# Second-group queries placed between the halves of the group one scores, norm sums accumulated by the adds, and nine value steps placed anew

## The chip, the cores and the metric

The kernel runs on one core of one Trainium2 chip. A core has a matrix engine (TensorE, PE in the profile; its weight loads are PEld), a vector engine (VectorE, DVE), a scalar engine (ScalarE, ACT), GpSimd (POOL) and SyncE (SP), whose queue issues the DMAs here. The metric is the device time of one execution in microseconds. A profile is taken of one execution; its span runs from the first to the last instruction.

## What is computed

Two layers of the same block, for four sequences that each decode one token. A block is grouped-query attention over a cache of 4096 positions, then a gated feed-forward network, each behind a layer norm and with a residual.

```python
B, Sq, D = 4, 1, 512
Hq, Hkv, Sk, Dh = 32, 8, 4096, 128            # w_gate, w_up: 512 x 1792; all bf16
def _A_ref(x, k_cache, v_cache, wq, wo):
    q = (x @ wq)                               # 32 heads of 128; 4 query heads share a key head
    scores = einsum("bhqd,bhkd->bhqk", q, k) * (Dh ** -0.5)
    o = einsum("bhqk,bhkd->bhqd", softmax(scores), v)
    return o @ wo
def _B_ref(x, w_gate, w_up, w_down):
    return (_gelu(x @ w_gate) * (x @ w_up)) @ w_down
x = x + _A_ref(_layernorm(x), K, V, wq, wo);  x = x + _B_ref(_layernorm(x), ...)
x = x + _A_ref(_layernorm(x), K, V, wq, wo);  x = x + _B_ref(_layernorm(x), ...)
```

Both layers use the same caches and the same weights. The keys are 33.6 MB and the values 33.6 MB.

## The kernel before

**Stages.** The order of all instructions is written by hand (`manual_schedule`), so what is written first on an engine runs first on it. The first layer's attention goes row by row over the four sequences. The main loop (L624 to L646) has one pass for each row b: the dense stage of the first layer for row b, the norm and queries of the second layer for row b, and then `attend` (L461), which joins the second layer's attention of row b with the first layer's attention of row b+1. In the last pass `attend_last` (L567) has only the second layer's part. A final dense stage does all four rows at once (L648).

**Groups and tiles.** The eight key heads form two groups of four (`groups`, L113; ga comes first, gb second). A cache tile is half the positions of one head, 128 x 2048 bf16, 512 KB. All 16 key tiles of a row stay in SBUF in `KT`, and both layers use them, so keys are read from HBM once. `keys.load` (L333) overwrites a tile with that of the next row; on SP's queue it waits until the second layer's scores have read it. `keys.turn` (L340) transposes each tile in place, on VectorE. `scores` (L351) takes one half (t) of one group: 16 matmuls against `qb`, which `q_build` (L230 on TensorE, L233 on VectorE) fills for one group at a time. `q_rows` (L209) is the query product of a group, 16 matmuls; its rows are transposed by L199 and spread by `q_spread` (L220).

**Values.** Values are read for each layer anew, into seven buffers. A value step (`Values.step`, L432) uses one tile in 16 matmuls (L446), gives its buffer back, and lets `load_v` (L426) put further loads on SP's queue. The order of use is written down in `order`: the second layer's first two tiles of a row (kept in their buffers since the first layer, KEEP), 16 tiles of the next row's first layer, then the other 14 of the second layer. Those 14 steps are left over when `attend` returns; the next pass spends them as `fill(n)` in the dense stage and `rest(n)` in `attend`. While `seen["hold"]` is set, `load_v` issues nothing. In `attend` this keeps value loads behind the key loads on SP's queue.

**Small pieces.** The norm squares x (L154), averages x and its square over partitions with a matmul (L159), reduces the four columns (L161), subtracts the mean (L162), and finds the reciprocal root in ten small steps on VectorE (`ln_rstd`). The dense stage has two input products (`ffn_in`, L285), the gate (`gelu`, `gate_up`, with H_bf at L308) and the down product (L315). `soft` (from L357) is the softmax of a group: maximum, exponential (L370), and then a transpose (L378), 16 products (L397) and a copy to `pe` (L400).

## Time and profile before

| | |
|---|---|
| median of 8 runs | 324.69 us (321.93 to 327.6) |
| the profiled execution | 323.01 us, span 321.2 us |
| moved by DMA | 110.38 MB on SP's queue |
| HBM rate over the span | 344 GB/s |
| mean granted TensorE clock | 0.714 |
| value loads | 112 into value buffers, 8 into key tiles |
| key loads | 64 |

The page shows the span in 40 slices of 8 us. Each digit is a busy share in tenths; the last row is the rate in GB/s.

```profile
PE   1460576334675369879854488998444888976964
...
DVE  5576750023458894254488943544789434533134
...
DMA  6999999999949999998999999999999999899910
GB/s 250 399 412 406 407 410 396 350 387 374 361 118 406 400 396 330 302 376 285 285 414 408 411 406 385 338 318 319 403 411 409 406 395 344 266 327 357 406 41 3
```

From left to right: the first row's attention up to about 50 us, then the weights' loading, and from 84 us on the main loop. The low slice at 88 to 96 us lies between the dense stage of row 0 and the first loads of the next row's keys. Similar, shallower places come near 150, 210 and 280 us. The last two slices are the final dense stage, with nothing left to load.

### The profile page before, as it was taken

Reading aid. Unit: us, or ns where it says so; the run is one execution under the profiler, and the core shown is the slowest. Engines: PE = TensorE matmul, PEld = TensorE weight load, DVE = VectorE, ACT = ScalarE, POOL = GpSimd, SP = SyncE. Lnnn points to the kernel's source line nnn. Section 1 sums busy time; section 2 is a strip of 40 time slices with the busy share of each in tenths; the row PEclk is TensorE's granted clock in tenths of the full one; section 3 lists DMA queues with packets and bytes.
Section 4 is the critical chain, followed back from the end, with each engine's and each line's share of the span. In section 5 each row is a group of like instructions: output and inputs, shape, how many; then the busy total and the mean of one; then the engine's idle time right before and its main releaser. Section 6 shows DMA issues by size and latency. Waiting matters only on the chain.

```text
span 321.2 us, 8609 instructions
## 1 busy us (share of the span) xinstructions
PE 208.5 (65%) x3812; PEld 120.6 (38%) x3812; DVE 172.1 (54%) x459; ACT 29.0 (9%) x70; POOL 0.7 (0%) x6
## 2 busy tenths in 40 slices
PE   1460576334675369879854488998444888976964
PEld 0010245121332046645520256665202565635542
DVE  5576750023458894254488943544789434533134
ACT  0002010000010103000201012001011120004000
POOL 0000000000000000000000000000000000000000
PEclk9999999999997555576955555559555555578557
DMA  6999999999949999998999999999999999899910
GB/s 250 399 412 406 407 410 396 350 387 374 361 118 406 400 396 330 302 376 285 285 414 408 411 406 385 338 318 319 403 411 409 406 395 344 266 327 357 406 41 3
DMA packets 34646, 110.94 MB, mean 345 GB/s; under 512 B 3112, under 2 KB 9008, under 8 KB 34608
## 3 DMA queue, kind: packets, MB, share of 16 engines
q1 hardware_dynamic: 34608, 110.38, 92.2%
q8 instruction: 30, 0.49, 0.6%
q14 instruction: 8, 0.07, 0.0%
HBM read 110.37 MB, written 0.00 MB: 344 GB/s over the span
## 4 chain that ended last, share of the span: by engine, by line
DMA 58%; PE 25%; DVE 7%; SPq 6%; issue 2%; ACT 1%; ACTq 0%
DMA kt<-in_A_k_cache_dram 25%; DMA v<-in_A_v_cache_dram 25%; PE sc L351 7%; PE ot L446 6%; DMA wd_sb<-in_B_w_down_dram 5%; PE rows L209 3%; DMA kt<-in_A_v_cache_dram 3%; DVE kt L340 3%; SPq L126 3%; PE rows L285 2%; PE y L315 2%; PE rows L264 2%; SPq L333 1%; PE y L270 1%; SPq L127 1%
## 5 line engine op out<-in xcount | busy, mean ns | idle before, releaser
L340 DVE STREAM_TRANSPOSE kt<-kt 128x1024 f32<-128x1024 f32 x64 | 76.2, 1223 | 9.4 <-DMA kt<-in_A_k_cache_dram 8.9
L446 PEld LDWEIGHTS <-v 128*128 128x128 bf16 x1920 | 60.4, 104 | 54.7 <-DMA v<-in_A_v_cache_dram 30.6
L446 PE MATMUL ot<-pe,v 128*128 128x4 bf16 x1920 | 64.3, 166 | 23.5 <-DMA v<-in_A_v_cache_dram 19.9
L351 PE MATMUL sc<-kt,qb 128*32 128x512 bf16 x512 | 59.8, 518 | 20.9 <-DVE kt L340 18.3
L351 PEld LDWEIGHTS <-qb 128*32 128x32 bf16 x512 | 17.2, 110 | 49.1 <-issue 24.5
L199 DVE STREAM_TRANSPOSE rows<-rows 128x512 f32<-128x512 f32 (+1 forms) x25 | 17.5, 702 | 27.2 <-PE rows L264 15.2
L453 DVE TENSOR_TENSOR OT_bf<-ot,rden 128x8 bf16<-128x8 f32 x32 | 5.4, 170 | 41.6 <-PE ot L446 34.9
L370 ACT ACTIVATE pp<-sc,nm 128x512 bf16<-128x512 f32 x16 | 11.0, 688 | 157.2 <-DVE junk L366 127.7
L397 PE MATMUL x<-pp,ident_bf 128*32 128x128 bf16 x256 | 9.1, 283 | 23.3 <-DVE pp L378 23.2
L209 PE MATMUL rows<-wq_sb,xn_bf 128*1 128x512 bf16 (+1 forms) x160 | 17.5, 589 | 5.3 <-DMA wq_sb<-in_A_wq_dram 4.7
L264 PE MATMUL rows<-wo_sb,OT_bf 128*1 128x512 bf16 (+1 forms) x120 | 14.8, 614 | 6.6 <-DMA wo_sb<-in_A_wo_dram 6.3
L397 PEld LDWEIGHTS <-ident_bf 128*32 128x32 bf16 x256 | 6.7, 121 | 29.4 <-issue 27.3
L357 DVE TENSOR_REDUCE m<-sc 128x1 f32<-128x512 f32 x16 | 10.8, 675 | 12.6 <-PE sc L351 12.6
L378 DVE STREAM_TRANSPOSE pp<-pp 128x512 bf16<-128x512 bf16 x16 | 11.2, 702 | 5.6 <-ACT pp L370 5.3
L233 DVE TENSOR_TENSOR qb<-qe,amask 128x256 bf16<-128x256 f32 x16 | 6.8, 422 | 10.2 <-PE qe L230 10.2
L400 ACT CAST pe<-x 128x512 bf16<-128x512 f32 x16 | 9.4, 586 | 21.9 <-PE x L397 21.9
L315 PE MATMUL y<-H_bf,wd_sb 128*128 128x1 bf16 (+1 forms) x280 | 8.2, 165 | 3.9 <-DVE H_bf L308 2.3
L285 PE MATMUL rows<-wg_sb,xn_bf 128*1 128x448 bf16 (+1 forms) x80 | 8.3, 567 | 3.0 <-DMA wg_sb<-in_B_w_gate_dram 2.4
L285 PE MATMUL rows<-wu_sb,xn_bf 128*1 128x448 bf16 (+1 forms) x80 | 8.1, 556 | 2.9 <-DMA wu_sb<-in_B_w_up_dram 2.9
L315 PEld LDWEIGHTS <-wd_sb 128*128 128x128 bf16 x280 | 7.8, 102 | 5.6 <-DMA wd_sb<-in_B_w_down_dram 3.5
L276 DVE TENSOR_TENSOR XX<-XX,y 128x4 f32<-128x4 f32 (+1 forms) x10 | 1.6, 160 | 15.5 <-PE y L315 9.1
L230 PE MATMUL qe<-qm,t_bf 128*128 128x64 bf16 x16 | 3.3, 208 | 9.1 <-DVE rden L388 5.0
(66 smaller groups left out, 122.5 us busy)
## 6 DMA issues: line engine op xcount, KB each, us to landing
v<-in_A_v_cache_dram SPq DMA_DIRECT2D x112, 512.0 KB, 8.3
kt<-in_A_k_cache_dram SPq DMA_DIRECT2D x64, 512.0 KB, 10.5
wq_sb<-in_A_wq_dram SPq DMA_DIRECT2D x2, 2048.0 KB, 11.2
wo_sb<-in_A_wo_dram SPq DMA_DIRECT2D x4, 1024.0 KB, 11.9
kt<-in_A_v_cache_dram SPq DMA_DIRECT2D x8, 512.0 KB, 9.3
wg_sb<-in_B_w_gate_dram SPq DMA_DIRECT2D x1, 1792.0 KB, 13.5
wu_sb<-in_B_w_up_dram SPq DMA_DIRECT2D x1, 1792.0 KB
wd_sb<-in_B_w_down_dram SPq DMA_DIRECT2D x2, 896.0 KB, 16.6
```

Source lines behind the costliest of these rows:

```text
L199: nc.vector.transpose(out=rows[:, :n], in_=rows[:, :n])
L209: nc.tensor.matmul(rows[j * QS:j * QS + nb, :], lhsT=xn_bf[:, k, bs], rhs=w, start=(k == 0), stop=(k == KD - 1))
L264: nc.tensor.matmul(rows[r0:r0 + lhsT.shape[-1], :], lhsT=lhsT, rhs=wo_sb[:, i, :], start=(at == 0 and n < QD), stop=(at == 2 and n >= hp - ...
L285: nc.tensor.matmul(rows[j * QS:j * QS + nb, :KF * QS], lhsT=xn_bf[:, k, bs], rhs=w[:, j], start=(k == 0), stop=(k == KD - 1))
L315: nc.tensor.matmul(y[:, k], lhsT=wd_sb[:, c, k * P:(k + 1) * P], rhs=H_bf[:, c, :], start=(c == 0 and k == 0), stop=(c == KF - 1), skip_gr ...
L340: nc.vector.transpose(out=words, in_=words)
L351: nc.tensor.matmul(sc[s * QS:(s + 1) * QS], lhsT=qb[:, w0:w0 + 2 * W], rhs=kt[:, :, be // 2, :, be % 2], start=(t == 0 and be == 0), stop= ...
L357: nc.vector.tensor_reduce(out=m[:], in_=sc.rearrange("p c j -> p (c j)"), axis=AX.X, op=ALU.max)
L370: nc.scalar.activation(out=pp[:], in_=sc[:], func=ACT.Exp, bias=nm[:, 0:1], scale=scale, accum_out=ls[:])
L378: nc.vector.transpose(out=flat, in_=flat)
L397: nc.tensor.matmul(x[a * QS:(a + 1) * QS, s], lhsT=ident_bf[:, s * QS:(s + 1) * QS], rhs=pT[:, a], start=True, stop=True, skip_group_check ...
L446: nc.tensor.matmul(self.ot[:, s % 2], lhsT=v[:, i, :], rhs=pe[:, s, c, :], start=(c == 0), stop=(c == C - 1), skip_group_check=True)
```

## The change

The change has three parts. It moves work and leaves the amounts of scores, values and loads as they were.

- **Order.** `last_q`, which built the second group's `qb` behind both halves of the group ga scores, becomes `next_q`: the product of the second group's queries (L209) and what follows it are no longer issued in the main loop but between the two halves of the group ga scores, with `q_build` behind the second half. The hold is set before the first scores. It stops only tiles of the next row's first layer; the second layer's own tiles may still load. The 14 left-over value steps were 10 ahead of `attend` (6 in `dense`, 4 behind it) and 4 in it; they are now 9 (5 and 4) and 5. In the dense stage both input products follow each other, two steps stand ahead of the down product and one behind it. Behind the first group's query product there are two steps, and one more behind its `q_build`.
- **Norm sums.** For one row, the add and the square become `scalar_tensor_tensor` with `accum_out`, so that the matmul of the norm averages two columns. The mean is read as a scalar from its result, and a copy to `mv` stands behind the subtraction.
- **Buffers.** `p1p`, the pool of the first layer's `pe`, has one buffer instead of two. A tile `sums` of two columns is added.

```diff
-    p1p = ctx.enter_context(tc.tile_pool(name="p1p", bufs=NG))
+    p1p = ctx.enter_context(tc.tile_pool(name="p1p", bufs=1))
...
     def ln_square(b0, nb):
         bs = slice(b0, b0 + nb)
-        nc.vector.tensor_tensor(out=XX[:, 1, bs], in0=XX[:, 0, bs], in1=XX[:, 0, bs], op=ALU.mult)
+        if nb == 1:
+            nc.vector.scalar_tensor_tensor(out=XX[:, 1, b0], in0=XX[:, 0, b0], scalar=1.0,
+                                           in1=XX[:, 0, b0], op0=ALU.mult, op1=ALU.mult,
+                                           accum_out=sums[:, 1:2])
+        else:
...
     def ln_center(b0, nb):
         bs = slice(b0, b0 + nb)
+        mv = small.tile([P, 2, nb], FP32, name="mv", tag="mv")
+        if nb == 1:
+            st = ps_sm.tile([P, 2, 1], FP32, name="st", tag="sm")
+            nc.tensor.matmul(st.rearrange("p s o -> p (s o)"), lhsT=mean_f[:, :], rhs=sums[:],
+                             start=True, stop=True)
+            nc.vector.tensor_scalar(out=xn_bf[:, :, b0], in0=XX[:, 0, b0], scalar1=st[:, 0],
+                                    scalar2=None, op0=ALU.subtract)
+            nc.vector.tensor_copy(out=mv[:], in_=st[:])
+            return mv
...
     def add_y(b0, nb, y):
         bs = slice(b0, b0 + nb)
...
+        if nb == 1:
+            nc.vector.scalar_tensor_tensor(out=XX[:, 0, b0], in0=XX[:, 0, b0], scalar=1.0,
+                                           in1=y[:, :, 0], op0=ALU.mult, op1=ALU.add,
+                                           accum_out=sums[:, 0:1])
+        else:
...
     def load_v():
-        while not seen["hold"] and free and seen["load"] < seen["upto"]:
-            b, g, s, t = loads[seen["load"]]
+        while free and seen["load"] < seen["upto"]:
+            b, last, g, s, t = loads[seen["load"]]
+            if seen["hold"] and not last:
+                return
...
         if two:
...
-            for t in range(NT):
-                scores(sc2[0], ga, t)
-                keys.load(GH)
-            last_q()
             seen["hold"] = True
-            rest(2)
+            scores(sc2[0], ga, 0)
+            keys.load(GH)
+            qm1 = next_q()
+            scores(sc2[0], ga, 1)
+            keys.load(GH)
+            q_build(qm1, gb)
+            rest(1)
             for t in range(NT):
                 scores(sc2[1], gb, t)
                 keys.load(GH)
-            rest(1)
             seen["hold"] = False
             load_v()
             p0 = soft(sc2[0])
-            rest(1)
+            rest(2)
             soft_turn(p0)
             pe0, den0 = soft_swap(p0, p2p), soft_den(p0)
+            rest(2)
...
-    def attend_last(b2, last_q, rest):
+    def attend_last(b2, next_q, rest):
...
-        for t in range(NT):
+        def freed(t):
             scores(sc2[0], ga, t)
             free[:0] = [KT[ga * GH + s][t] for s in range(GH)]
             load_v()
-        last_q()
-        rest(2)
+
+        freed(0)
+        qm1 = next_q()
+        freed(1)
+        q_build(qm1, gb)
+        rest(1)
         p0 = soft(sc2[0])
         for t in range(NT):
             scores(sc2[1], gb, t)
         rest(2)
         soft_turn(p0)
         prob2[ga] = (soft_swap(p0, p2p), soft_recip(soft_den(p0)))
+        rest(2)
...
     def dense(b0, nb, proj, fill):
         out_proj_end(*proj)
         y = proj[0]
+        fill(1)
         add_y(b0, nb, y)
         ln_square(b0, nb)
-        fill(1)
         mv = ln_center(b0, nb)
         fill(1)
         rg = ffn_in(b0, nb, wg_sb)
-        rstd = ln_rstd(nb, mv)
-        sq, h = gelu(nb, rg, rstd)
+        ru = ffn_in(b0, nb, wu_sb)
+        sq, h = gelu(nb, rg, ln_rstd(nb, mv))
+        H_bf = gate_up(nb, sq, h, ru)
+        fill(2)
+        y = down(nb, H_bf)
         fill(1)
-        ru = ffn_in(b0, nb, wu_sb)
-        H_bf = gate_up(nb, sq, h, ru)
-        fill(3)
-        y = down(nb, H_bf)
         add_y(b0, nb, y)
...
         dense(b, 1, proj, fill)
         ln_square(b, 1)
-        fill(1)
         mv = ln_center(b, 1)
         fill(1)
+        ga, gb = groups(b + 1)
+        qr0 = q_rows(b, 1, ga)
         rstd = ln_rstd(1, mv)
...
-        ga, gb = groups(b + 1)
-        qr0 = q_rows(b, 1, ga)
+        qm0 = q_spread(turn_rows(qr0, 512)[:, :, 0], am, ga)
+        fill(2)
+        q_build(qm0, ga)
         fill(1)
-        qm0 = q_spread(turn_rows(qr0, 512)[:, :, 0], am, ga)
-        qr1 = q_rows(b, 1, gb)
-        fill(1)
-        q_build(qm0, ga)
-        qm1 = q_spread(turn_rows(qr1, 512)[:, :, 0], am, gb)
+
+        def next_q():
+            return q_spread(turn_rows(q_rows(b, 1, gb), 512)[:, :, 0], am, gb)
+
         if b < B - 1:
-            proj, prev = attend(b, b + 1, lambda: q_build(qm1, gb), fill)
+            proj, prev = attend(b, b + 1, next_q, fill)
         else:
-            proj = attend_last(b, lambda: q_build(qm1, gb), fill)
+            proj = attend_last(b, next_q, fill)
```

More of the change, by code (lines that the diff above doesn't have):

```diff
@@ L94 @@
     XX = state.tile([P, 2, B, KD], FP32, name="XX")
+    sums = state.tile([P, 2], FP32, name="sums")
     OT_bf = state.tile([P, Hq], BF16, name="OT_bf")
@@ L153, in ln_square @@
         bs = slice(b0, b0 + nb)
-        nc.vector.tensor_tensor(out=XX[:, 1, bs], in0=XX[:, 0, bs], in1=XX[:, 0, bs], op=ALU.mult)
+        if nb == 1:
[3 more added lines that the diff above has]
+        else:
+            nc.vector.tensor_tensor(out=XX[:, 1, bs], in0=XX[:, 0, bs], in1=XX[:, 0, bs],
+                                    op=ALU.mult)
     def ln_center(b0, nb):
         bs = slice(b0, b0 + nb)
+        mv = small.tile([P, 2, nb], FP32, name="mv", tag="mv")
[7 more added lines that the diff above has]
+            return mv
         st = ps_sm.tile([P, 2, nb, KD], FP32, name="st", tag="sm")
         nc.tensor.matmul(st[:], lhsT=mean_f[:, :], rhs=XX[:, :, bs], start=True, stop=True)
-        mv = small.tile([P, 2, nb], FP32, name="mv", tag="mv")
         nc.vector.tensor_reduce(out=mv[:], in_=st[:], axis=AX.X, op=ALU.add)
@@ L275, in add_y @@
         bs = slice(b0, b0 + nb)
-        nc.vector.tensor_tensor(out=XX[:, 0, bs], in0=XX[:, 0, bs],
-                                in1=y.rearrange("p k b -> p b k"), op=ALU.add)
+        if nb == 1:
[3 more added lines that the diff above has]
+        else:
+            nc.vector.tensor_tensor(out=XX[:, 0, bs], in0=XX[:, 0, bs],
+                                    in1=y.rearrange("p k b -> p b k"), op=ALU.add)
     def ffn_in(b0, nb, w_sb):
@@ L415 @@
     assert all(u in keep for u in [(0,) + w[2:] for w in value_order(0, 0)[VB - KEEP:]])
-    loads = [(u[0],) + u[2:] for u in order if not (u[1] and (u[0],) + u[2:] in keep)]
+    loads = [u for u in order if not (u[1] and (u[0],) + u[2:] in keep)]
     free = [kvin.tile([P, CH, Dh], BF16, name=f"v{i}") for i in range(KV_BUFS)]
@@ L459, in pairs, with attend @@
         return [(order[n][2] * GH + order[n][3] // 2 * 2) * rep for n in range(0, VB, 2 * NT)]
-    def attend(b2, b1, last_q=None, rest=None):
+    def attend(b2, b1, next_q=None, rest=None):
         two, first = b2 is not None, b1 == 0
```

## The prediction

> **What bounds the kernel now.** First the page, for the bound; then the busy time by stretches, for where that bound is not reached; then the timeline of one such place. A "pass" is one turn of the loop over the four batch rows (row 0 to 3).
>
> ```profile
> PE 208.5 (65%) x3812; PEld 120.6 (38%) x3812; DVE 172.1 (54%) x459; ACT 29.0 (9%) x70; POOL 0.7 (0%) x6
> ...
> q1 hardware_dynamic: 34608, 110.38, 92.2%
> ...
> DMA 58%; PE 25%; DVE 7%; SPq 6%; issue 2%; ACT 1%; ACTq 0%
> ...
> v<-in_A_v_cache_dram SPq DMA_DIRECT2D x112, 512.0 KB, 8.3
> ```
>
> The cache stream bounds it: 110.38 MB, and 58% of the chain that ended last. In its good stretches it runs at about 410 GB/s, 1.28 us for a 512 KB tile. The stretches (last three columns: granted clock, DMA share, GB/s) show where it doesn't:
>
> ```profile
> 176.00:180.00 4.00, 1.77 (x35) 1.41 (x34) 3.58 (x7) 1.34 (x4) 0.00 (x0) 0.50 1.03 409
> 204.00:208.00 4.00, 4.00 (x62) 1.53 (x60) 2.93 (x16) 0.21 (x1) 0.00 (x0) 0.50 0.96 345
> 208.00:212.00 4.00, 3.87 (x126) 3.73 (x123) 1.39 (x6) 0.00 (x0) 0.00 (x0) 0.50 0.92 315
> 212.00:216.00 4.00, 3.96 (x61) 1.74 (x65) 2.92 (x15) 0.00 (x0) 0.00 (x0) 0.52 0.96 305
> 220.00:224.00 4.00, 3.35 (x84) 2.20 (x81) 1.96 (x8) 1.09 (x3) 0.00 (x0) 1.00 0.90 275
> 276.00:280.00 4.00, 3.85 (x61) 1.99 (x62) 2.83 (x16) 0.00 (x0) 0.00 (x0) 0.50 0.78 225
> ```
>
> From 204 to 216 (dense stage, pass of row 2) TensorE is full and DMA is at three quarters: five free value buffers come back only as TensorE uses them, and the next row's keys can't load before scores of the second layer have read their tiles. That point ends the stretch:
>
> ```profile
> 209.46 1.63 PE L315 MATMUL y<-H_bf,wd_sb 128*128 128x1 bf16 x56
> 212.65 1.87 PE L209 MATMUL rows<-wq_sb,xn_bf 128*1 128x512 bf16 x16
> 214.97 1.47 PE L209 MATMUL rows<-wq_sb,xn_bf 128*1 128x512 bf16 x16
> 217.52 2.05 PE L351 MATMUL sc<-kt,qb 128*32 128x512 bf16 x32 [0.54 <-DVE qb L233]
> 218.64 17.12 SPq L333 DMA_DIRECT2D kt<-in_A_k_cache_dram  x16
> 226.35 1.25 DVE L340 STREAM_TRANSPOSE kt<-kt 128x1024 f32<-128x1024 f32 x1 [2.03 <-DMA kt<-in_A_k_cache_dram]
> 283.81 3.41 PE L351 MATMUL sc<-kt,qb 128*32 128x512 bf16 x32 [0.54 <-DVE qb L233]
> ```
>
> To see: both query products precede the first score; key loads start 1.1 us after it. These loads start at 90.94, 153.72 and 218.64; in the last pass (values into key tiles) at 285.53. The spacings, 62.8, 64.9 and 66.9 us, carry 46 tiles each (16 key, 30 value), 58.9 us at 1.28. So 4, 6 and 8 us a pass are open; nothing else here is worth as much.
>
> **Part 1, queries and value steps.** Second-group products go behind the first half of the group one scores, and nine value steps instead of ten stand ahead of it, elsewhere. Pass of row 2, by the timeline. The two L285 blocks (1.66 each) now follow each other, ending near 207.1; two value steps (0.5 each, tiles landed at 205 and 206.4) fill to 208.1. The down product needs H_bf, and that hangs on the DVE chain: from xn_bf (ends 204.0) to H_bf (ends 209.03) is 5.0, of which 0.34 waited for the second L285; the chain without it, plus a copy of 0.2 that the norm edit adds, gives H_bf at about 208.7. Down starts 0.75 earlier than 209.46. From xn_bf of the second norm to the first score it was 4.9 (212.60 to 217.52). It becomes the reciprocal-root chain 2.2, copy 0.2, transpose 0.73, spread 0.22, TensorE product 0.25 and L233 0.42: 4.05, 0.85 saved; the L209 block (1.47 to 1.87) and one value step (0.5) leave the path, so DVE is what is left on it. With 0.2 to 0.4 gained about the norms, key loads start 2.0 us earlier. Pass of row 1: the same order, and it now waits 1.9 us for values (0.49, 0.72, 0.68 idle at 141.6, 142.9, 144.1) in three steps in a row that are spread out: 3.5 earlier. Pass of row 3: a value wait of 1.54 at 282.67 also goes: 3.8 earlier. Row 0 has no value steps to place: 0.85 less the norm edit, 0.6.
>
> Every value step brings its DMA issue. SP's queue holds, in order, four key loads, then (after 1.5 to 1.8 us of L209 and 1.0 of scores) four more, then eight. Four tiles are 5.1 us of transfer and the last values are still on their way, so that hole is covered; if only two were, it would cost about 1 us. The hold now begins earlier, but nine steps free exactly what the pass's last values need (5 + 9 = 14 tiles), so the next layer's first value tile, until now loaded ahead of the keys, comes behind them. Its 1.28 us is given back in each of passes 1 to 3. Can the freed buffers feed the new bunches of two? A value tile lands 5.6 to 8.5 us after its issue at 200 to 218 us; the step pair after the first-group product uses tiles issued 6 us before. Taking 6 (median 6.6), the price is 0 to 0.6; at 8.5 it is 2.
>
> Clock: the row of 283.81 has 3.41 us for 32 scores, where the granted clock was 0.54; the row of 217.52 has 2.05, at 1.00. In this kernel the clock rose at 215.4 and 151 while two L209 blocks ran nearly back to back. The Trainium skill (TensorE: Matmul & The Clock Gate, section "Part 1: The HAM clock gate") says that full clock is granted after a window of about 3.4 us of sustained activity. The trace agrees only where wide matmuls follow each other: 204 to 215 is full of instructions and stays at 0.50. (The L285 blocks, now adjacent, may raise the clock, but 8 us ahead of the scores; a rise at 140.4 was over by 144.6.) With the blocks parted, by the rule read as "busy" the scores keep 2.05 and cost nothing; by the row they cost 0.7 in the half ahead of the key loads, in passes 1 and 2 (pass 3 pays already, pass 0 is at 1.00). I take 0.5, nearer to the row.
>
> What I can't see is the start of the key stream: 220 to 224 ran at 275 GB/s just as 16 key issues pile up, and 288 to 292 at 265. Parted issues could ease it, up to 1.4 us a pass, or leave it; I count 0.3.
>
> **Part 2, norm sums.** Eight one-row norms. The nearest row for the accumulating form is L366: 163 ns and an 82 ns read-out, twice per norm. The 167 ns reduce leaves xn_bf's path; xn_bf takes a pointer scalar (L633: 228 against 169), and a copy (L245: 175) moves behind it. The matmul of two columns instead of eight is priced like L159, 357. Sum per norm on the way to xn_bf: +164 - 197 + 59, nothing; on the root chain +0.2, counted above. Bounds: -0.2 to +0.2 a norm.
>
> **Part 3, one p1p buffer.** The second group's copy must wait for the first group's eight value steps; these stand ahead of its 16 L397 products on TensorE, so the wait is over: zero. If that order did not hold, it would cost at most the 0.59 of L400 per pass.
>
> **Sum.** Key loads earlier, less the value tile, the clock, and plus the start: row 1: 3.5 - 1.3 - 0.5 + 0.3 = 2.0; row 2: 2.0 - 1.3 - 0.5 + 0.3 = 0.5; row 3: 3.8 - 1.3 - 0 + 0.3 = 2.8, of which I drop 1.0, as DMA ran at 225 at 276 to 280 without a reason I can name. Row 0's 0.6 is lost to rival A. Together 4.3; less 0.3 for value waits, 4.0. The final dense stage (308 to the end, 3 GB/s) keeps its order and saves nothing. The profiled execution took 323.01 (span 321.2): 319.0. The median of the runs is 324.69, 1.7 above it; the forecast for the median is 320.7.
>
> **Rivals.** A: the gain is swallowed by DVE. The first group's softmax now stands behind the second L209 block and behind L233 of the second group, 1.5 us later after the first score. On DVE it precedes all key transposes (64 of 1.22), which run nearly full: in row 0's pass 21.3 busy of 24 us (96 to 120). Against: before the first transpose DVE waited for its tile 0.72 (row 1) and 2.03 (row 2). In row 0's pass 0.45 and 0.56 of waits further on absorb most. If this eats the earlier start, the net is 0 to -2: 323 to 324.7.
>
> B: slower. Same place, one price: the scores drop to half clock and the first score is not earlier, because the bunched value steps wait for tiles (8.5 us landings). Then softmax begins 1.7 + 1.8 + 1.7 = 5.2 after the first score instead of 2.05, so the first key transpose slips by 3.2 less the 0.72 or 2.03 of slack, and the last pass slips its exponentials too: 2.5 + 1.2 + 1.5, with 0.3 in row 0: 5.5, 330. It decides where the first score comes less than about 1.2 us earlier (row 2) or 2.5 (row 1). Against: the DVE chain above gives 2.0 and 3.5.
>
> C: the steps weren't moved into gaps, since TensorE has none at 204 to 216, and the value supply sets the pace: no change, 324 to 325.
>
> **How the numbers follow.** The count as made: 0.57, 317.5 to 322.7, mostly beyond 1%. A and C together: 0.26, within 1%. B: 0.12, slower. A stronger gain than counted (start of the key stream eased as well): 0.05, 315 to 317. The range 317.0 to 326.0 leaves out B and the strongest gain. About 1% (3.2 us) is what a measurement of this kernel tells from no change. Faster by over 1%: 0.45 of the first case and 0.05: 0.50; slower 0.12; within 1% 0.38.
>
> **What would show it.** Right: first key loads of the passes some 2 to 4 us earlier after the first value step of the dense stage; the spacings near 63 instead of 65 to 67; DMA above 345 GB/s in the dense stage. Clock: L351 blocks of 16 at 1.0 or 1.7 us, at 1.00 or 0.50. A: the first L340 of a pass starts with no wait for its DMA. B: value steps idle for DMA between L209 and L351. Part 2 is wrong if L276 with its read-out takes more than 0.3. The forecast as a whole is wrong if the spacings shrink but V waits after 120, 185 and 250 grow by as much.

## The result, and the profile after

| | before | after |
|---|---|---|
| median | 324.22 us (318.65 to 327.6, 32 runs) | 318.82 us (317.27 to 322.12, 11 runs) |
| profiled execution | 323.01, span 321.2 | 318.83, span 317.0 |
| mean granted TensorE clock | 0.714 | 0.702 |

The ratio is 0.9911, with a 95% interval from 0.9876 to 0.9947. It counts, of each kernel, only the runs within 1.5% of its own fastest one (13 of the 32 before, 10 of the 11 after), while the medians count all, so it is nearer to 1 than the ratio of the medians (0.983). The kernel is faster, by 0.5 to 1.2% on that ratio. The forecast was 320.7 for the median, with a range of 317.0 to 326.0.

The page of the changed kernel, in its first parts: busy shares, slices of 7.9 us, the DMA queue, and the chain of work that ended last.

```profile
PE 211.1 (67%) x3812; PEld 121.1 (38%) x3812; DVE 170.2 (54%) x475; ACT 28.9 (9%) x70; POOL 0.7 (0%) x6
...
PE   1460585343576667899954588999645788897864
...
DVE  5575751014348895454498933544889344534133
...
GB/s 256 384 412 396 411 409 403 350 379 383 392 112 365 407 407 312 312 358 330 351 405 408 410 408 406 365 283 359 414 409 409 407 388 347 290 291 415 404 46 3
...
q1 hardware_dynamic: 34608, 110.38, 92.5%
...
DMA 49%; PE 21%; DVE 18%; SPq 6%; issue 3%; ACT 1%; ACTq 0%
...
v<-in_A_v_cache_dram SPq DMA_DIRECT2D x112, 512.0 KB, 8.3
```

The bytes are the same and the low places of the last row are still there: 312 near 119 to 135, 283 near 206 to 214, and 290 and 291 near 270 to 285. VectorE's share of the chain went from 7% to 18%. Stretches of the passes of row 2 and row 3 show the same places closer (columns: stretch in us, its length, busy time of PE, PEld, DVE, ACT and POOL with their counts, then granted clock, DMA share, GB/s):

```profile
204.00:208.00 4.00, 3.59 (x113) 3.05 (x105) 1.84 (x11) 0.21 (x1) 0.00 (x0) 0.50 0.79 283
208.00:212.00 4.00, 3.65 (x66) 2.11 (x66) 2.98 (x16) 0.00 (x0) 0.00 (x0) 0.50 0.83 258
212.00:216.00 4.00, 3.86 (x49) 1.76 (x53) 0.49 (x2) 0.00 (x0) 0.00 (x0) 0.50 1.00 355
220.00:224.00 4.00, 2.71 (x90) 2.32 (x83) 1.82 (x4) 1.42 (x4) 0.00 (x0) 0.96 1.01 387
276.00:280.00 4.00, 3.42 (x65) 1.86 (x66) 1.43 (x4) 0.00 (x0) 0.00 (x0) 0.50 0.86 274
```

From 204 to 212, which is the dense stage before its first score, the stream runs at 258 to 283 GB/s: no better than before. The stretch of 220 to 224 runs at 387 instead of 275, but it lies 5.2 us behind the first key load here and 1.4 us behind it before; stretches cut at the first key load follow further down. The gain is not where the kernel is slowest; it is behind it. The timeline of the pass of row 2:

```profile
205.70 1.65 PE L335 MATMUL y<-H_bf,wd_sb 128*128 128x1 bf16 x56 [0.28 <-DVE H_bf L328]
208.83 1.88 PE L224 MATMUL rows<-wq_sb,xn_bf 128*1 128x512 bf16 x16
212.87 1.90 PE L371 MATMUL sc<-kt,qb 128*32 128x512 bf16 x16
214.56 1.92 PE L224 MATMUL rows<-wq_sb,xn_bf 128*1 128x512 bf16 x16
214.79 16.24 SPq L353 DMA_DIRECT2D kt<-in_A_k_cache_dram  x16
216.26 1.35 PE L371 MATMUL sc<-kt,qb 128*32 128x512 bf16 x16
218.29 1.99 PE L371 MATMUL sc<-kt,qb 128*32 128x512 bf16 x32
223.14 1.23 DVE L360 STREAM_TRANSPOSE kt<-kt 128x1024 f32<-128x1024 f32 x1
```

One query product precedes the first score, the other stands between the two halves. The first half of the scores takes 1.90 us for 16 matmuls, where 32 took 2.05 before, so the key loads start 1.92 us after the first score and not 1.12. The first key transpose has no wait in brackets: VectorE comes later than its tile.

A ledger of the whole span, worked out from the two timelines. A pass is cut at the end of the output product (L270 before, L285 after) and at its first key load (in the last pass: the first value load into a key tile). In the lines of rows 1 to 3, the first number is output product to key load, the second is key load to the next output product.

| us | before | after | difference |
|---|---|---|---|
| start to output product of row 0 | 69.82 | 70.14 | +0.32 |
| row 0: output product to key load | 21.12 | 21.46 | +0.34 |
| row 0: key load to next output product | 45.03 | 45.12 | +0.09 |
| row 1 | 17.75 / 48.77 | 14.63 / 48.50 | -3.12 / -0.27 |
| row 2 | 16.15 / 48.76 | 14.94 / 49.33 | -1.21 / +0.57 |
| row 3 (second part: to the end) | 18.13 / 35.67 | 15.64 / 37.24 | -2.49 / +1.57 |

Key loads come 6.82 us earlier over three passes, 1.87 of it is given back behind them and 0.75 is lost up to row 1: 4.20, the difference of the spans. Behind the key loads one value tile more has to be carried in each of these passes (nine value loads precede them, not ten). Three tiles would be 3.84 us at 1.28. That less is given back is mainly due to the first 10 us of the key stream. Before:

```profile
153.72:163.72 10.00, 7.04 (x166) 4.63 (x158) 4.76 (x13) 1.67 (x4) 0.00 (x0) 0.87 0.98 314
218.64:228.64 10.00, 6.30 (x164) 4.39 (x155) 4.52 (x13) 1.67 (x4) 0.00 (x0) 0.87 0.96 331
285.53:295.53 10.00, 7.64 (x179) 4.85 (x171) 4.25 (x15) 2.76 (x7) 0.00 (x0) 0.84 0.93 318
```

And after:

```profile
151.35:161.35 10.00, 7.86 (x189) 4.93 (x182) 5.45 (x16) 1.67 (x4) 0.00 (x0) 0.97 1.00 368
214.79:224.79 10.00, 8.00 (x171) 4.62 (x164) 5.03 (x14) 1.67 (x4) 0.00 (x0) 0.84 1.00 372
279.76:289.76 10.00, 8.89 (x207) 5.49 (x200) 5.01 (x17) 2.08 (x5) 0.00 (x0) 0.84 0.99 345
```

Against the 410 GB/s of a good stretch, 10 us at 314, 331 and 318 lose 2.3, 1.9 and 2.2 us of transfer; at 368, 372 and 345 they lose 1.0, 0.9 and 1.6. That is 3.0 us over the three passes; the 3.84 less these 3.0 would give back 0.86, so about 1.0 us more is lost somewhere else, and the ledger does not say where.

Counted in transfer, the start weighs even more. From output product to key load the kernel before had:

```profile
135.97:153.72 17.75, 15.01 (x305) 9.15 (x306) 9.27 (x45) 0.21 (x1) 0.00 (x0) 0.67 0.94 333
202.49:218.64 16.15, 15.17 (x305) 9.25 (x306) 9.26 (x45) 0.21 (x1) 0.00 (x0) 0.59 0.96 341
267.40:285.53 18.13, 15.74 (x306) 9.19 (x306) 9.26 (x45) 0.21 (x1) 0.00 (x0) 0.59 0.91 320
```

That is 17.2 MB in 52.0 us, and 14.8 MB in 45.2 us after (348, 320 and 312 GB/s, shown below). Against 410 GB/s, 10.0 us of transfer were lost there before and 9.2 after. So of the 6.82 us by which the keys come earlier, only 0.8 is transfer that is no longer lost; the rest, 4.7 tiles, is carried later. That is more than the three tiles counted above, and the 1.0 us can have gone there. The start of the key stream brings 3.0 of the 4.20. Both are read from one execution of each kernel.

### The profile page after: what moved, and what is told of

It is laid out like the page before. It is cut to its first block, busy times and chain, and to the rows that moved or that the text cites. A ratio compares the mean times of both kernels' runs of the same rounds, so it can differ in the third digit from the quotient of the medians.

```text
span 317.0 us, 8624 instructions
## 1 busy us (share of the span) xinstructions
PE 211.1 (67%) x3812; PEld 121.1 (38%) x3812; DVE 170.2 (54%) x475; ACT 28.9 (9%) x70; POOL 0.7 (0%) x6
## 4 chain that ended last, share of the span: by engine, by line
DMA 49%; PE 21%; DVE 18%; SPq 6%; issue 3%; ACT 1%; ACTq 0%
DMA v<-in_A_v_cache_dram 25%; DMA kt<-in_A_k_cache_dram 15%; PE sc L371 6%; DMA wd_sb<-in_B_w_down_dram 5%; DVE kt L360 5%; PE ot L468 5%; DMA kt<-in_A_v_cache_dram 3%; SPq L127 3%; PE y L335 2%; PE rows L224 2%; DVE rows L214 2%; PE rows L279 2%; DVE qb L248 1%; PE st L168 1%; PE x L417 1%
## 5 line engine op out<-in xcount | busy, mean ns | idle before, releaser
L468 PEld LDWEIGHTS <-v 128*128 128x128 bf16 x1920 | 59.8, 104 | 47.7 <-DMA v<-in_A_v_cache_dram 24.3
L468 PE MATMUL ot<-pe,v 128*128 128x4 bf16 x1920 | 63.5, 166 | 20.4 <-DMA v<-in_A_v_cache_dram 17.0
L360 DVE STREAM_TRANSPOSE kt<-kt 128x1024 f32<-128x1024 f32 x64 | 74.1, 1211 | 4.0 <-DMA kt<-in_A_k_cache_dram 4.0
L371 PE MATMUL sc<-kt,qb 128*32 128x512 bf16 x512 | 63.0, 540 | 15.7 <-DVE kt L360 14.0
L371 PEld LDWEIGHTS <-qb 128*32 128x32 bf16 x512 | 17.0, 115 | 46.5 <-issue 37.0
L224 PE MATMUL rows<-wq_sb,xn_bf 128*1 128x512 bf16 (+1 forms) x160 | 18.5, 610 | 4.8 <-DMA wq_sb<-in_A_wq_dram 4.4
L279 PE MATMUL rows<-wo_sb,OT_bf 128*1 128x512 bf16 (+1 forms) x120 | 14.8, 614 | 6.8 <-DMA wo_sb<-in_A_wo_dram 6.6
L305 PEld LDWEIGHTS <-xn_bf 128*1 128x1 bf16 (+1 forms) x160 | 4.6, 113 | 13.3 <-issue 12.1
```

Source lines behind the costliest of these rows:

```text
L224: nc.tensor.matmul(rows[j * QS:j * QS + nb, :], lhsT=xn_bf[:, k, bs], rhs=w, start=(k == 0), stop=(k == KD - 1))
L279: nc.tensor.matmul(rows[r0:r0 + lhsT.shape[-1], :], lhsT=lhsT, rhs=wo_sb[:, i, :], start=(at == 0 and n < QD), stop=(at == 2 and n >= hp - ...
L305: nc.tensor.matmul(rows[j * QS:j * QS + nb, :KF * QS], lhsT=xn_bf[:, k, bs], rhs=w[:, j], start=(k == 0), stop=(k == KD - 1))
L360: nc.vector.transpose(out=words, in_=words)
L371: nc.tensor.matmul(sc[s * QS:(s + 1) * QS], lhsT=qb[:, w0:w0 + 2 * W], rhs=kt[:, :, be // 2, :, be % 2], start=(t == 0 and be == 0), stop= ...
L468: nc.tensor.matmul(self.ot[:, s % 2], lhsT=v[:, i, :], rhs=pe[:, s, c, :], start=(c == 0), stop=(c == C - 1), skip_group_check=True)
```

## The experiments

Three questions: which part of the change pays; what eases the start of the key stream; and whether the new order has room left. "Start" below is the rate in the first 10 us from the first key load, for rows 1, 2 and 3.

### The norm sums, taken out and put in alone

The first kernel is the changed one with the old norm, the second is the kernel before with the new norm and the one `p1p` buffer. Of the first one's edit, the add (the square and the mean go back in the same way):

```diff
...
     def add_y(b0, nb, y):
         bs = slice(b0, b0 + nb)
-        if nb == 1:
-            nc.vector.scalar_tensor_tensor(out=XX[:, 0, b0], in0=XX[:, 0, b0], scalar=1.0,
-                                           in1=y[:, :, 0], op0=ALU.mult, op1=ALU.add,
-                                           accum_out=sums[:, 0:1])
-        else:
-            nc.vector.tensor_tensor(out=XX[:, 0, bs], in0=XX[:, 0, bs],
-                                    in1=y.rearrange("p k b -> p b k"), op=ALU.add)
+        nc.vector.tensor_tensor(out=XX[:, 0, bs], in0=XX[:, 0, bs],
+                                in1=y.rearrange("p k b -> p b k"), op=ALU.add)
```

> The changed kernel without the norm edit: the add, the square, the four-column average and the reduce as before; the order and the one p1p buffer as changed. My reading (the norm edit is worth nothing on the path): within 0.3% of the changed kernel, so about 0.988 of the kernel before by the medians (318.8 to 320). Rival (the edit gives the gain, as it shortens the chain to xn_bf in eight norms): 1 us or more slower than the changed kernel, 320 to 322. A third: the read-outs and the copy cost 0.2 a norm on the root chain, then this is 1 to 1.5 us faster, 317.5.

> The kernel before with the norm edit and the one p1p buffer alone, order as before. My reading: no change, 0.997 to 1.003 of the kernel before. The rival that the norm sums carry the gain expects 0.99. Were the single p1p buffer a wait, it would be slower by up to 0.6 us in each of four passes, 1.007.

Order alone: 319.37 us (6 runs; the kernel before had 324.41 there), ratio 0.9851 (0.9786 to 0.9917). Within its interval that is the whole gain. Norms alone: 323.53 (17 runs) against 324.41, ratio 0.9899 (0.9856 to 0.9942). Here medians and ratio disagree: the medians are 0.3% apart, as I expected, and the ratio, which rests on 8 of the 17 runs, says 1%, as the rival did. Since the change without the norm sums loses nothing, I read them as worth nothing in the new order; that they help in the old one isn't excluded.

### The second product back ahead of the scores, and the product alone moved

The first of these is the changed kernel with both query products back to back:

```diff
         qr0 = q_rows(b, 1, ga)
+        qr1 = q_rows(b, 1, gb)
...
-            return q_spread(turn_rows(q_rows(b, 1, gb), 512)[:, :, 0], am, gb)
+            return q_spread(turn_rows(qr1, 512)[:, :, 0], am, gb)
```

> The changed kernel with the second group's L209 block put back directly behind the first group's, ahead of all scores; the value steps and all else as changed. Clock: with the blocks paired the L351 blocks of the second layer's first group should run at about 1.0 us per half again (1.9 in the changed kernel) and the granted clock be 1.00 there. Time, theory 1 (the changed kernel gains because its key loads go out in parted bunches, so that the key stream starts at a higher rate): the two halves are again 1 us apart, the 10 us from the first key issue fall back from 0.9 to 1.6 us of lost transfer to 1.9 to 2.4, and 2 to 4 us of the gain go: 321 to 323. Theory 2 (it gains because the first score comes earlier): the product adds 1.5 ahead of it and the clock gives 0.85 back, so 0.6 a pass, 2 us in all: 320.5 to 321, with the key stream starting as in the changed kernel.

It took 322.76 (22 runs; the kernel before 324.41), ratio 1.0005 (0.9977 to 1.0034): by the ratio nothing of the gain is left, by the medians 1.7 of 5 us. And not for late keys, which in sum are no later: they start 14.57, 15.91 and 14.65 us behind the output product, against 14.63, 14.94 and 15.64. In rows 1 and 3 the clock is at 1.00, and they follow the first score in 1.09 us instead of 1.92. The stretches from output product to key load of this kernel:

```profile
136.36:150.93 14.57, 13.83 (x290) 8.53 (x290) 9.04 (x48) 0.21 (x1) 0.00 (x0) 0.72 0.90 314
201.70:217.61 15.91, 15.04 (x289) 8.94 (x290) 9.03 (x48) 0.21 (x1) 0.00 (x0) 0.61 0.85 272
269.20:283.85 14.65, 13.92 (x290) 8.44 (x290) 9.04 (x48) 0.21 (x1) 0.00 (x0) 0.71 0.86 292
```

And of the changed kernel:

```profile
136.72:151.35 14.63, 13.47 (x273) 8.24 (x274) 8.17 (x46) 0.21 (x1) 0.00 (x0) 0.62 0.97 348
199.85:214.79 14.94, 13.92 (x273) 8.68 (x274) 8.16 (x46) 0.21 (x1) 0.00 (x0) 0.50 0.90 320
264.12:279.76 15.64, 13.98 (x274) 8.70 (x274) 8.17 (x46) 0.21 (x1) 0.00 (x0) 0.50 0.89 312
```

With the same nine value loads, the stream runs at 314, 272 and 292 GB/s instead of 348, 320 and 312. In transfer lost against 410 that is 13.0 us instead of 9.2 over three passes. The 1.9 us product stands ahead of three value steps, so their buffers come back later: counted from the output product, the last three value loads ahead of the keys begin to be issued at 12.55, 13.01 and 12.62 us in the three rows, against 11.09, 11.40 and 12.11 in the changed kernel. Its place matters for the buffers more than for the first score. Late buffers need not be all of it: in row 2 the DMA share of 0.85 would carry 349 GB/s at the 410 of a full stream, and 272 were moved, so the packets took longer too.

The other one is the kernel before with only the product moved between the halves (value steps, hold and norm as they were):

```diff
-            for t in range(NT):
-                scores(sc2[0], ga, t)
-                keys.load(GH)
-            last_q()
+            scores(sc2[0], ga, 0)
+            keys.load(GH)
+            qm1 = last_q()
+            scores(sc2[0], ga, 1)
+            keys.load(GH)
+            q_build(qm1, gb)
...
```

> The kernel before with one thing changed: the second group's L209 block, its transpose and its spread stand between the two halves of the group ga scores, its q_build behind them. Ten value steps, their places, the hold and the norms as before. The run with the products paired lost 4 of the 5.5 us, so if the parts add up, this one alone carries them: 320 to 321 (0.988 to 0.991 of the kernel before). Rival (it only gains together with the value steps, which then free their buffers without a second product in between): the first score comes 1.5 us earlier in three passes, the half clock gives 0.85 back, and the softmax comes 1 us later after the first score: 322.5 to 324 (0.994 to 1.0).

320.06 (6 runs; the kernel before 323.62), ratio 0.9887 (0.9828 to 0.9945). This one step of the change brings 3.6 us by the medians, where the changed kernel on the same chip brings 4.7. Key loads come 1.2 and 2.2 us earlier in rows 1 and 3, and 0.2 later in row 2. Its start is eased as in the changed kernel (366, 345 and 374):

```profile
153.97:163.97 10.00, 8.43 (x179) 4.87 (x172) 5.38 (x15) 1.67 (x4) 0.00 (x0) 0.84 0.99 366
217.45:227.45 10.00, 8.42 (x165) 4.69 (x158) 5.01 (x14) 1.67 (x4) 0.00 (x0) 0.80 1.00 345
281.97:291.97 10.00, 8.46 (x195) 5.34 (x187) 4.75 (x16) 2.13 (x5) 0.00 (x0) 0.96 1.01 374
```

### What eases the start: the key issues, or distance between the halves

The kernel before with only the places of its key loads on SP's queue changed: four behind the first half of group one, four behind the first half of group two and eight behind its second half. The last pass (row 3) is not touched.

```diff
-            for t in range(NT):
-                scores(sc2[0], ga, t)
-                keys.load(GH)
+            scores(sc2[0], ga, 0)
+            keys.load(GH)
+            scores(sc2[0], ga, 1)
             last_q()
...
-            for t in range(NT):
-                scores(sc2[1], gb, t)
-                keys.load(GH)
+            scores(sc2[1], gb, 0)
+            keys.load(GH)
+            scores(sc2[1], gb, 1)
+            keys.load(2 * GH)
```

> The kernel before, with only the place of key loads on SP's queue changed: four behind the first half of the group ga scores as before, the next four behind the first half of the second group (2 to 3 us later instead of 1), the last eight behind its second half. Scores, queries, norms and value steps as before. Theory 1 (piled key issues slow the start of the stream): the lost transfer in the 10 us from the first key issue falls from 2.2 to about 1.2 in each of the first three passes, 2 to 3 us in all, 0.990 to 0.994 of the kernel before. Theory 2 (the start is slow for another reason, scores running at the same time or fewer tiles under way): no change, or slower by up to 1 us as keys come later: 0.998 to 1.003.

323.41 (22 runs), ratio 0.9989 (0.9961 to 1.0018). The start is 312 and 317 GB/s in rows 1 and 2: no better than 314 and 331. (The 284 of row 3 belongs to an order that is as before, where the first profile had 318: so much can one place vary.) The edit also brings the later keys later, and the DMA share is 0.91 and 0.93 instead of 0.98 and 0.96; but even at a full share, an estimate from these rows, the rates would be 343 and 341, against 368 and 372 in the changed kernel. So parting the issues, by which I had argued for the easing in the forecast, does not bring it about. In this profile the clock was 0.50 at the first scores in all three rows, so a slow first half alone does not ease the start either.

Then the kernel before with two value steps put between the halves, in the place where the change has the product (the hold set earlier, so that they issue no load):

```diff
-            for t in range(NT):
-                scores(sc2[0], ga, t)
-                keys.load(GH)
+            seen["hold"] = True
+            scores(sc2[0], ga, 0)
+            keys.load(GH)
+            rest(2)
+            scores(sc2[0], ga, 1)
+            keys.load(GH)
             last_q()
-            seen["hold"] = True
-            rest(2)
...
```

> The kernel before with one thing changed: the two value steps that stood behind the last scores of the first group now stand between its two halves (both query products stay ahead of the first score, back to back; the hold is set before the scores, so the steps issue no load there, as before). Question: why the start of the key stream is eased (10 us from the first key issue lose 0.9 to 1.6 us of transfer where the second product stands between the halves, 1.9 to 2.4 in the kernel before, and 2.3 to 3.1 with only the places of the key issues changed). Theory 1, mere distance: what counts is that the first eight key tiles are not asked for within 2 us while the last values still arrive. Then the two steps (about 1 us of TensorE) between the halves ease it too, to 1.0 to 1.7 us lost, and the time falls by 1 to 2 us, to about 322. Theory 2, the product: what counts is that one product less stands ahead of the first score, so that the first key issue comes at a better time against the last values. Then the loss stays at 1.9 to 2.6 and the time at 323 to 324.5.

324.48 (22 runs; the kernel before 323.88), ratio 0.9996 (0.9965 to 1.0028), and a start of 329, 327 and 328. About a microsecond of other work between the halves is not enough. What is left is the product: one that is no longer ahead, or one (1.9 us) that is between. The runs don't part these two. The kernel with the products paired ahead of the scores starts at 347, 359 and 358, within what the moved product shows: so something in the other edits eases the start as well, or the dip has only moved out of the 10 us that are looked at.

### Fewer steps ahead, with the products paired in the gap

The changed kernel with both products ahead, where value steps had stood, and two of the nine steps moved behind the group one scores, so that TensorE has less ahead of them.

```diff
             scores(sc2[0], ga, 1)
             keys.load(GH)
+            rest(2)
             q_build(qm1, gb)
...
         qr0 = q_rows(b, 1, ga)
+        qr1 = q_rows(b, 1, gb)
...
-        fill(2)
         q_build(qm0, ga)
...
```

> The changed kernel with both L209 blocks paired again, but in the place of the two value steps that stand behind the first block; these two go behind the group ga scores. So seven value steps instead of nine stand ahead of the first score. If the first score is bound by the VectorE chain (about 4.0 us from xn_bf), it stays where it is in the changed kernel or comes 0.5 later, with the clock at 1.00 and both halves done within 2.1 us. Theory A (when the key loads go out, and the clock, decide): key issues 0.5 earlier, softmax 2 us earlier, 0.5 to 1 us a pass, 316 to 318. Theory B (value buffers that come free ahead of the key issue decide, since only transfers that are under way by then count): two frees later, each pass loses 0.5 to 1.5 us, 320.5 to 323, with more transfer lost between the output product and the key issue than in the changed kernel (2.2 to 3.7 us).

339.24 (6 runs; before 323.62), ratio 1.0506 (1.0453 to 1.0558): far worse. The first score came as early as hoped (13.23, 13.15 and 12.87 us behind the output product). In the pass of row 1 of its timeline:

```profile
150.63 5.56 SPq L353 DMA_DIRECT2D kt<-in_A_k_cache_dram  x8
...
158.15 1.61 SPq L448 DMA_DIRECT2D v<-in_A_v_cache_dram  x2
160.71 9.29 SPq L353 DMA_DIRECT2D kt<-in_A_k_cache_dram  x8
168.37 0.58 PE L468 MATMUL ot<-pe,v 128*128 128x4 bf16 x16 [11.58 <-DMA v<-in_A_v_cache_dram]
...
170.52 1.23 DVE L360 STREAM_TRANSPOSE kt<-kt 128x1024 f32<-128x1024 f32 x1
```

The second layer's last two value tiles are issued behind eight key loads, at 158.15. TensorE works in order and stops 11.58 us at the step that needs the first of them, and the first key transpose starts 19.9 us behind the first key load (7.93 in the changed kernel). Nine steps ahead of the scores, with five free buffers, are exactly the 14 tiles of the second layer. Nine can't be seven.

### Room in the changed kernel

Ahead of the down product TensorE idles 0.28 us for H_bf. One step moved there, from behind the first query product (nine in all, as before the edit):

```diff
-        fill(2)
+        fill(3)
         y = down(nb, H_bf)
...
-        fill(2)
+        fill(1)
         q_build(qm0, ga)
```

> The changed kernel with one value step moved: three instead of two ahead of the down product, one instead of two behind the first query product (nine ahead of the scores, as before this edit). In the changed kernel TensorE idles 0.28 to 0.36 us ahead of the down product for H_bf. Theory 1, that idle time is real room: the step fills it, its buffer comes back some 3 us earlier, and key loads start up to 0.3 us earlier per pass: 318 to 318.9, a ratio to the changed kernel of 0.997 to 1.0. Theory 2, the chain: the step is 0.5 us, 0.2 longer than the room, so down and the second norm come 0.2 us later, and the idle time moves to behind the first query product, where TensorE then waits for VectorE's spread: no change or up to 0.3 us later per pass, 319 to 320.

321.88 (21 runs; the kernel before 323.88), ratio to the kernel before 0.9949 (0.9919 to 0.9978), where the changed kernel has 0.9911: worse than both expectations. The profiled execution took 324.44, so only its order of work is read, in row 2:

```profile
208.31 1.55 PE L335 MATMUL y<-H_bf,wd_sb 128*128 128x1 bf16 x56
...
210.90 0.56 PE L168 MATMUL st<-sums,mean_f 128*128 128x2 f32 x2 [0.63 <-DVE XX L156]
...
214.94 0.24 PE L245 MATMUL qe<-qm,t_bf 128*128 128x64 bf16 x1 [0.72 <-DVE qm L235]
215.97 0.58 PE L468 MATMUL ot<-pe,v 128*128 128x4 bf16 x16 [0.80 <-DMA v<-in_A_v_cache_dram]
```

The wait for H_bf is gone, and others have grown behind it: 0.63 for the norm (none in row 2 of the changed kernel) and 0.72 for the spread (0.47 there), and alike in rows 1 and 3; in row 2 there is also 0.80 for a value tile. The idle time was not room; it only went elsewhere. How much of the loss of time that explains is not shown. The start was 326, 345 and 322 GB/s although the product stands between the halves; since this execution was one of the longest, that decides nothing.

The changed kernel was run twice more, on other chips, for its own spread:

> The changed kernel again, on the chip of the two beside it, as their measure: 318 to 320.

318.94 (6 runs; before 323.62), ratio 0.9879 (0.9828 to 0.9929); start 382, 398 and 386 GB/s, better than in the first profile.

> The changed kernel itself once more, on the same chip as the kernel with row 0's products paired, to compare the two directly and to have a third profile of the start of the key stream. Both theories: 318 to 319.5, 10 us from the first key issue lose 0.3 to 1.6 us of transfer in rows 1 to 3; a profile with more than 2 us lost there would say that the eased start is not a property of this order but varies from run to run.

318.96 (6 runs; before 324.64), ratio 0.9847 (0.9796 to 0.9899); start 394, 403 and 332 GB/s. The 332 loses 1.9 us, more than the 1.6 expected: the eased start varies from run to run with the same order.

Last, row 0 alone with both products ahead. Row 0 has no value steps, and the ledger has its key loads 0.34 us later than before.

```diff
+        if b == 0:
+            qr1 = q_rows(b, 1, gb)
...
+        if b == 0:
+            qm1 = q_spread(turn_rows(qr1, 512)[:, :, 0], am, gb)
...
+            if b == 0:
+                return qm1
             return q_spread(turn_rows(q_rows(b, 1, gb), 512)[:, :, 0], am, gb)
```

> The changed kernel, but in the pass of row 0 alone the second group's query product is issued as in the kernel before: right behind the first group's, both ahead of the first score (row 0 has no value steps to place, so nothing else differs). Question: was row 0's pass made worse by the change (rival A of the forecast, VectorE as the bound, and the half clock in the first half of its scores), or is it neutral? Theory 1, rival A holds in row 0: there VectorE runs full behind the first key tiles; the softmax of the first group comes 1.5 us later in the changed kernel (first key transpose 6.55 us behind the first key issue instead of 4.48), and the next output product ended 0.75 us later (136.72 against 135.97). Then this kernel ends that product near 136.0 and is 0.7 to 1.0 us faster than the changed one: about 318.0, ratio to it 0.997. Theory 2, slack takes it up: VectorE waited 0.45 and 0.56 us for its tiles in the kernel before, the start of the key stream is worse by 0.4 us with the products back to back; the time stays within 0.3 us of the changed kernel's.

317.66 (6 runs), ratio to the kernel before 0.9808 (0.9764 to 0.9853), 1.3 us under the changed kernel on the same chip; but the next output product ended at 137.54, not near 136.0. So the time was there without its reason, and it was run again:

> The changed kernel with row 0's two query products back to back, once more: does its 317.66 (1.3 us under the changed kernel on the same chip) hold, and where does it come from? The first profile had the time but not the place: row 0's pass, from the end of its output product to the end of the next, took 66.9 us, against 66.6, 66.0 and 67.7 in three profiles of the changed kernel. Theory 1, row 0's pass is really shorter: the median is again 317 to 318.2 (the changed kernel: 318.82, 318.94, 318.96), and this profile's pass of row 0 takes under 66.0. Theory 2, chance: 318.5 to 319.2.

319.59 (6 runs; before 323.48), ratio 0.9892 (0.9855 to 0.9929), with 66.4 us for row 0's pass. The 1.3 us didn't hold. VectorE's first key transpose came 4.5 us behind the first key load in both runs, 2.0 earlier than in the changed kernel, and the time did not follow.

No kernel tried beats the changed one by more than it varies itself.

## Why the forecast held, and which of its terms were off

The forecast for the profiled execution was 319.0 and it took 318.83; the 1.7 us put on for the median was not needed (the profiled execution of the changed kernel lies at its median). The order of things was foreseen: in rows 1 to 3 the first score and the key loads come earlier, and that wins more than the deferred tile costs. But most of the net gain is in a term that the forecast had counted among the smallest, the start of the key stream. That the sum is met so closely is luck: the start of the key stream gave 2.1 us more than forecast, and the clock, the stretch up to row 1 and what is left over took 2.3 of it away again, while single executions of the changed kernel lie between 317.27 and 322.12. Term by term, over the three passes of rows 1 to 3:

| us | forecast | measured |
|---|---|---|
| first score earlier (row 1 / 2 / 3) | 3.5 / 2.0 / 3.8, and 1.0 dropped | 3.94 / 2.01 / 2.69 |
| half clock in the first half | -0.5 / -0.5 / 0 | -0.82 / -0.80 / -0.20 |
| value tile behind the keys | -3.84 | -3.84 + 2.98 - 1.01 |
| start of the key stream eased | +0.9 | (2.98 of the line above) |
| value waits | -0.3 | (in the 1.01) |
| up to row 1 | 0 | -0.75 |
| sum | 4.0 | 4.20 |

The 1.01 is no measurement; it is what is left when all else is counted.

- **First score.** The VectorE chain was read rightly: 2.01 us for row 2, and no value wait stands on its way. Row 3 fell 1.1 short, about the 1.0 that I had dropped without a reason. The timeline has most of the reason, a value wait at the start of its dense stage, which also puts its first score 0.70 behind row 2's (13.72 and 13.02 from the output product):

```profile
265.78 0.58 PE L468 MATMUL ot<-pe,v 128*128 128x4 bf16 x16 [0.54 <-DMA v<-in_A_v_cache_dram]
```

- **Clock.** The mechanism held, the size didn't: 0.8 us in rows 1 and 2, and in row 0 as well, for which I had counted nothing. The chip's own record doesn't show it there (see below). The Trainium skill (TensorE: Matmul & The Clock Gate, "Part 1: The HAM clock gate") asks for a window of sustained activity; from 204 to 216 TensorE is busy 3.59 to 3.86 us of each 4 and stays at 0.50. The row, not the rule read as "busy", gave the right sign.
- **The start of the key stream** is the term that failed by most: 0.3 us a pass forecast, 1.3, 1.0 and 0.7 measured. In six profiles with this order in rows 1 to 3 (three of the changed kernel, one without the norm sums, two with row 0 paired) the start is 374 GB/s in the mean, with rows from 332 to 403, against 321 in the one profile of the kernel before: 1.3 us a pass. Its reason was wrong too: parting the issues alone did nothing (323.41), moving the product did (320.06). Why the product does it is open.
- **What was open.** The reading that each of the three spacings carries 46 tiles was wrong for the first. It carries 16 key and 26 value tiles, 53.8 us at 1.28, so 9 us of its 62.8 were open, not 4; the sum does not use this number.

```profile
107.62 44.77 SPq L426 DMA_DIRECT2D v<-in_A_v_cache_dram  x26
```

- **Dense stage.** I expected more than 345 GB/s there. It is 348, 320 and 312 between output product and key load, before 333, 341 and 320. The stage got shorter, not fuller. The product paired again shows that its place decides how full it is.
- **What was costed at nothing.** The norm sums: shown by the kernel without them; L276 (now L292) and its read-out take 0.24 us, under the 0.3 that was named as a sign of being wrong. The one `p1p` buffer: never tried alone; it was in both kernels that show no loss. The final dense stage still ends at 3 GB/s.
- **Rival A** named as its sign a first key transpose without a wait. The sign is there, in every pass that has key transposes, and VectorE's share of the chain rose. Its price is not: the spacings of the first key loads fell from 62.8, 64.9 and 66.9 to 59.8, 63.4 and 65.0. The sign was badly chosen, since a wait that vanishes says only that the tile comes earlier than VectorE, not that VectorE then bounds the pass. In row 0 the last two experiments bring VectorE's start forward by 2.0 us and gain nothing that lasts.
- **Rival B** needed value steps that wait for tiles between L224 and L371. None does in rows 1 to 3. The run with seven steps ahead shows what a value step that waits there can cost: 15.6 us.
- **Rival C** is refuted by the interval.
- **The sign against the whole forecast** was value waits that grow by as much as the spacings shrink. They did not: TensorE's waits for value tiles fell from 19.9 to 17.0 us over the span.

## What to carry to other kernels

When a stream is held up by buffers that a matrix engine frees, ask of each moved block not only what it delays at its end but which buffer releases stand behind it: a product of 1.9 us put back ahead of three such releases cost two thirds of the gain here by the medians and all of it by the ratio, with the key loads in sum no later. Count the loads that must be issued before a queue turns to another stream; two issued too late cost 15.6 us here, three times what the change brings. An idle gap of 0.3 us on an engine is no room if the chain that ends it goes on behind it.

## What the runs showed of the hardware

- In row 0 the first 16 scores took 1.90 us between 89.7 and 91.6, where the granted clock in the record is 1.00, as in the kernel before, whose scores ran faster (1.12 us to the key load). With both products directly ahead (the last two kernels) it is 1.09 us again. So the recorded clock did not tell the pace of this block, which came 2.0 us behind the last wide product. The scores' durations in ns (least, median, most), after and before:

```profile
L371 PE MATMUL sc<-kt,qb x16: 607/628/632, 89.7 to 91.0; 128*32 128x512 bf16 x16
L351 PE MATMUL sc<-kt,qb x28: 381/396/412, 89.8 to 91.3; 128*32 128x512 bf16 x28
```

- Two products back to back don't always raise the clock: it was 1.00, 0.50 and 1.00 at the first scores of rows 1 to 3 in the kernel with the products paired. With one value step between them, as in the kernel before, it was 0.50 in all three rows where only the key loads were parted.
- At the start of the key stream the DMA engines are busy by the record (share 0.96 and 1.00 in row 2, before and after) while they move 331 and 372 GB/s; in a good stretch a share of 1.03 moved 409. Busy engines there take longer for the same bytes, and a share near 1 does not mean a full stream.
